# Attention start-up of a fused attention and expert kernel: exponentials from PSUM, q, v and probability loads and POOL steps in another order

## The chip, the cores and the metric

The kernel runs on one core of a Trainium2 chip. The metric is the device time of one execution in microseconds; three runs of the kernel before are shown, and their median counts.

## The reference

Three stages in float32, on 2304 tokens of 512 features.

```python
k_p = k.reshape(B, H, Sp, 8, D).mean(axis=3)      # B, H, S, D = 4, 8, 576, 64; Sp = 72
v_p = v.reshape(B, H, Sp, 8, D).mean(axis=3)
scores = scale * q @ k_p.T                          # scale = 1/sqrt(D)
attn = exp(scores - max); attn /= sum + 1e-9
x = attn @ v_p                                      # as (2304, 512)
for e in range(4): out += p[:, e] * (relu(x @ w1[e]) @ w2[e])   # p = domain_probs / their sum
a, b = out @ g_w1, out @ g_w2; result = (a * b @ w3) @ w_out
```

## The kernel before

Tokens are worked in 18 tiles of 128, three tiles to a block of 384. The first block's attention is the start-up: nothing of the experts can run before it. From then on the matmuls of expert 0 (units of one 128-column chunk of w1, made by `expert_h` and followed two units later by the matmuls with w2) fill TensorE, and the attention of the later blocks is spread between them as small pieces, in lists called `hooks`. `hooks[n]` runs after half-unit n: `hooks[0]` after unit 0, `hooks[2]` after unit 1, and so on.

The program is scheduled by hand: every engine executes its instructions in the order in which the Python code emits them, and waits in that order. `lead` (L640) is the start-up as a list of pieces. Its parts are:

- `warm(n)`: n transposes of the identity on TensorE, into a PSUM bank that nobody reads.
- `do_k` (`pool_k`, L415 to L420): VectorE sums eight rows of k, POOL multiplies by a mask. `do_kT` (`make_kT`, L428, L430): TensorE transposes, ScalarE evicts.
- `do_qT(t)` (`make_qT`): for the first three tiles TensorE transposes q (L479), VectorE (L482) or ScalarE (L484) evicts; for later tiles VectorE alone transposes (L487).
- `do_scores(t)` (L500): eight matmuls into two PSUM banks, four heads in each.
- `do_exps(t)`: per bank the maximum on VectorE (L512), then for tiles 0 and 1 the scaled negated maximum on VectorE (L514) and four exponentials on ScalarE straight from PSUM (L516); for tile 2 and all later ones a subtraction on VectorE (L518) and one exponential of 288 columns on ScalarE (L519).
- `do_normalise(t, eng)`: the sums on VectorE (L525 to L527), then the product with their reciprocals (L530), on POOL or VectorE.
- `do_v`: POOL pools a head of v with three additions (L440 to L442); heads 5 to 7 are pooled on TensorE (`pool_v_pe`, L448).
- `do_turn(t)` (`attn_T`): TensorE transposes the probabilities, four heads at a time (L539); ScalarE evicts (L545), for the second half of tile 2 VectorE (L543).
- `do_attend(0)` (L554): the matmuls with v; ScalarE and VectorE split the result in a high and a low part (L175, L176).
- `weight(eng)`: takes the oldest expert weight from a ring of four buffers, ScalarE writes its high part (L175), `eng` its low part (L176), and SP issues the load of the next weight into a free buffer (L194, L196).

All loads are issued by SP in program order. First come those in `first`: k of batch 0 in five pieces (L399), q tiles 0 to 2 (L457), v heads 0 to 7 (L404); then four expert weights, the domain probabilities (L1088), and as space allows q tiles 3 and 4 (L469) and k of batch 1. The probabilities are normalised by `probs` (L619 to L622) in `hooks[7]`.

Of the kernel before, what the change touches and what calls it, by code (L numbers as in the profile page):

```python
# [11 lines left out]
AF = mybir.ActivationFunctionType  # L12
ALU = mybir.AluOpType
AX = mybir.AxisListType
# [3 lines left out]
def fused_kernel(  # L18
# [16 lines left out]
    nc = tc.nc  # L35
    PSUM = bass.MemoryType.PSUM

    B, H, S, D = q.shape
    POOL = 8
    NK = S // POOL  # L40
    NT, DM = out.shape
    E, _, F = moe_w1.shape
    P = 128
# [10 lines left out]
    NCH = (NROW + P - 1) // P  # L54
    TAIL = NROW - (NCH - 1) * P
    assert D == 64 and H * D == DM and NB * BLK == NT and 2 * HB == S and TAIL <= P and KC == 4 and FC == 8
    LOGIT = 1.0 / (POOL * D ** 0.5)
# [10 lines left out]
    LEAD = 3  # L68
# [73 lines left out]
    dp = p_area[:, :NTILE * E].rearrange("p (t e) -> p t e", e=E)  # L142
# [184 lines left out]
    with tc.manual_schedule():  # L327
# [16 lines left out]
        def bank(name):  # L344
            turn[0] += 1
            return spare[(turn[0] - 1) % len(spare)](name)
# [46 lines left out]
        in_t, kb_t, kT_t, vp_t, qT_t, sc_t, e_t, sm_t, at_t = {}, {}, {}, {}, {}, {}, {}, {}, {}  # L393
# [29 lines left out]
        def make_kT(b, g0, g1):  # L423
            if g0 == 0:
                kT_t[b] = ap.tile([P, NCH * P], F32, tag="kT", name="kT")
            pt = bank("kT_ps")
            for c in range(g0, g1):
                nc.tensor.transpose(pt[:, (c - g0) * P:(c - g0 + 1) * P],  # L428
                                    kb_t[b][:, c].rearrange("p a d -> p (a d)"), ident)
            nc.scalar.activation(kT_t[b][:, g0 * P:g1 * P], pt[:, :(g1 - g0) * P], AF.Copy)  # L430

        def pool_v(b, h, eng):
            if h == 0:
# [39 lines left out]
        def make_qT(t):  # L473

            if t < LEAD:
                r = in_t.pop(("q", t))
                pt = bank("qT_ps")
                for hp in range(NP):
                    nc.tensor.transpose(pt[:, hp * P:(hp + 1) * P], r[:, hp * P:(hp + 1) * P], ident)  # L479
                qT = acc_lead[0][:, t, :].rearrange("p (a b) -> p a b", b=P)  # L480
                if t == 0:
                    nc.vector.tensor_copy(qT.rearrange("p a b -> p (a b)"), pt)  # L482
                else:
                    nc.scalar.activation(qT.rearrange("p a b -> p (a b)"), pt, AF.Copy)  # L484
            else:
                qT = ap.tile([P, NP, P], F32, tag="qT", name="qT", bufs=1)
                nc.vector.transpose(qT.rearrange("p h (j a) -> p h a j", a=4), in_t.pop(("qb", t)))  # L487
            qT_t[t] = qT
# [4 lines left out]
        def scores(t):  # L493
            qT = qT_t.pop(t)
            sc_t[t] = []
            for half in range(2):
                sc = bank("sc")
                for hp in range(2 * half, 2 * half + 2):
                    for off, n, b, s in segments(t * P, P):
                        nc.tensor.matmul(sc[off:off + n, (hp % 2) * W:(hp % 2 + 1) * W],  # L500
                                         qT[:, hp, off:off + n], kT_t[b][:, hp * W:(hp + 1) * W],
                                         start=True, stop=True)
                sc_t[t].append(sc)

        def exps(t):
            e = ap.tile([P, H, NK], F32, tag="e", name="e", bufs=3)
            mx = ap.tile([P, H], F32, tag="mx", name="mx")
            for half, sc in enumerate(sc_t.pop(t)):
                s3 = sc[:, :2 * W].rearrange("p (g j) -> p g j", j=NK)
                m = mx[:, half * G:(half + 1) * G]  # L510
                eh = e[:, half * G:(half + 1) * G]
                nc.vector.tensor_reduce(m, s3, axis=AX.X, op=ALU.max)  # L512
                if t < LEAD - 1:
                    nc.vector.tensor_scalar(m, m, -LOGIT, None, op0=ALU.mult)  # L514
                    for g in range(G):
                        nc.scalar.activation(eh[:, g], s3[:, g], AF.Exp, scale=LOGIT, bias=m[:, g:g + 1])  # L516
                else:
                    nc.vector.tensor_tensor(eh, s3, m.unsqueeze(2).broadcast_to([P, G, NK]), op=ALU.subtract)  # L518
                    nc.scalar.activation(eh, eh, AF.Exp, scale=LOGIT)  # L519
            e_t[t] = e  # L520

        def sums(t):

            sm_t[t] = ap.tile([P, H], F32, tag="sm", name="sm")
            nc.vector.tensor_reduce(sm_t[t], e_t[t], axis=AX.X, op=ALU.add)  # L525
            nc.vector.tensor_scalar(sm_t[t], sm_t[t], 1e-9, float(POOL), op0=ALU.add, op1=ALU.mult)
            nc.vector.reciprocal(sm_t[t], sm_t[t])  # L527

        def normalise(t, eng):
            eng.tensor_tensor(e_t[t], e_t[t], sm_t[t].unsqueeze(2).broadcast_to([P, H, NK]), op=ALU.mult)  # L530

        def attn_T(t, half):
            i, o = divmod(t, TPB)
            if o == 0:
                at_t[i, half] = ap.tile([P, G, BLK], F32, tag="at", name="at")
            e = e_t[t]
            pt = bank("at_ps")
            for g in range(G):
                nc.tensor.transpose(pt[:NK, g * P:(g + 1) * P], e[:, half * G + g, :], ident)  # L539
            src = pt[:NK].rearrange("p (g s) -> p g s", s=P)  # L540
            dst = at_t[i, half][:NK, :, o * P:(o + 1) * P]
            if t == LEAD - 1 and half:
                nc.vector.tensor_copy(dst, src)  # L543
            else:
                nc.scalar.activation(dst, src, AF.Copy)  # L545
# [44 lines left out]
        def do_k(b, on_pool=0):  # L590
            return [(("k", b, c), lambda c=c: pool_k(b, c, nc.gpsimd if c < on_pool else nc.vector)) for c in range(NCH)]

        def do_kT(b, cut=4):
            return [(None, lambda: make_kT(b, 0, cut)), (None, lambda: make_kT(b, cut, NCH))]

        def do_v(b, *engs):
            return [(("v", b, h), lambda h=h: pool_v(b, h, engs[h % len(engs)])) for h in range(H)]

        def do_qT(t):
            return [(("q" if t < LEAD else "qb", t), lambda: make_qT(t))] if t < NTILE else []  # L600

        def do_scores(t):
            return [(None, lambda: scores(t))]

        def do_exps(t):
            return [(None, lambda: exps(t))]

        def do_normalise(t, eng=nc.gpsimd):
            return [(None, lambda: sums(t)), (None, lambda: normalise(t, eng))]

        def do_turn(t):
            return [(None, lambda half=half: attn_T(t, half)) for half in range(2)]

        def do_attend(i):
            return [(None, lambda hp=hp: attend(i, hp)) for hp in range(NP)]
# [8 lines left out]
        def weight(eng):  # L624
            return [(None, lambda: stream.split(eng))]

        VE, GP = nc.vector, nc.gpsimd
        W0, W1, W2 = 14, 6, 6

        def warm(n):  # L630

            def f():
                pw = bank("warm")
                for _ in range(n):
                    nc.tensor.transpose(pw[:, :P], ident, ident)
            return [(None, f)]

        k0, kT0, k1, kT1 = do_k(0), do_kT(0), do_k(1, 3), do_kT(1, 3)
        v0 = do_v(0, GP)[:5] + [(None, lambda: pool_v_pe(0, 5))]
        lead = (warm(W0) + k0[:4] + kT0[:1] + k0[4:] + do_qT(0) + kT0[1:] + do_qT(1) + do_scores(0) + do_exps(0) + v0[:3]  # L640
                + do_qT(2) + do_scores(1) + do_exps(1) + do_scores(2) + do_normalise(0) + v0[3:4] + do_exps(2) + v0[5:]
                + do_normalise(1) + v0[4:5] + warm(W1) + do_turn(0) + do_normalise(2, VE) + warm(W2) + do_turn(1) + do_turn(2)
                + weight(GP) + do_qT(3) + k1[:3] + do_attend(0) + weight(VE))

        hooks = [[] for _ in range(2 * FC * ATT_BLOCKS + 11)]
        hooks[1] = k1[3:]
        hooks[7] = [(None, probs)]
        hooks[3] = kT1[:1] + do_qT(TPB + 1)
        hooks[4] = kT1[1:]
# [17 lines left out]
        for b, at_v, at_k, at_kT in ((1, 3, None, None), (2, 15, 15, 20), (3, 26, 25, 30)):  # L667
            for n, piece in enumerate(do_v(b, GP)):
                hooks[at_v + n].append(piece)
            if at_k:  # L670
                for n, piece in enumerate(do_k(b)):
                    hooks[at_k + n // 2].append(piece)
                hooks[at_kT] += do_kT(b)
        first = [("k", 0, c) for c in range(NCH)] + [("q", t) for t in range(LEAD)] + [("v", 0, h) for h in range(H)]
        loads += first + [what for what, _ in lead + sum(hooks, []) if what and what not in first]


# [407 lines left out]
            add_w2(0, n)  # L1085
        fetch(len(first))
        stream.fill()
        nc.sync.dma_start(dp, domain_probs.rearrange("(t p) e -> p t e", p=P))  # L1088
        soon = [("qb", TPB)] + [("k", 1, c) for c in range(NCH)] + [("qb", TPB + 1)]
        for piece in lead:  # L1090
            cooled(0)
# [225 lines left out]
        for half in range(2):  # L1317
            for n_b, b in enumerate(g_order):
# [29 lines left out]
                first, second = xo_t[0], xo_t[1]  # L1348
# [113 lines left out]
```

## Time and profile before

| | before |
|---|---|
| median of 3 runs | 1166.04 us (1165.78 to 1166.24) |
| profiled execution | 1165.1 us |
| its span | 1163.4 us |
| mean granted TensorE clock | 0.998 |
| busy: TensorE, VectorE, ScalarE, POOL | 1150.0, 796.7, 380.7, 484.4 us |
| DMA | 217.53 MB, mean 187 GB/s |

The span is what the profiler saw between the first and the last instruction; the time of the execution has 1.7 us around it. Times in rows are microseconds from the span's start. PE is TensorE, DVE VectorE, ACT ScalarE, SP the queue that issues DMAs. A busy TensorE is not one at its peak, as matmuls overlap.

### The profile page before, as it was taken

The numbers are of one execution on the slowest core, as the hardware profiler recorded it, in microseconds if no ns is written. First come the engines' busy times: TensorE is split into PE (matmuls) and PEld (weight loads), VectorE is DVE, ScalarE is ACT, GpSimd is POOL, SyncE is SP. The second block draws the span as 40 slices with busy tenths as digits, with TensorE's granted clock in tenths as the row PEclk, the third lists the DMA queues.
The fourth block names the chain that finished last, engine by engine and source line by source line (L and its number), as shares of the span: only waits on it lengthen the run. The fifth ranks groups of instructions, "written<-read, shape, count | busy, mean of one in ns | idle before, by whom it ended". The sixth has DMA issues, their size and how long they took to land.

```text
span 1163.4 us, 19411 instructions
## 1 busy us (share of the span) xinstructions
PE 1150.0 (99%) x6806; PEld 1041.1 (89%) x6806; DVE 796.7 (68%) x1624; ACT 380.7 (33%) x699; POOL 484.4 (42%) x563
## 2 busy tenths in 40 slices
PE   7999999999999999999999999999999999999998
PEld 6888898999898998998988989989889999999997
DVE  6866553476586778667778577877677777775454
ACT  4543433245141234421315414124352333231110
POOL 6965222166452547634446736255001222342111
PEclk9999999999999999999999999999999999999999
DMA  8956424555877645668583488686475542844651
GB/s 212 214 146 144 150 97 143 186 193 178 278 236 231 215 136 157 226 185 252 181 252 101 153 242 243 155 264 150 138 184 212 200 172 112 322 169 181 233 189 46
DMA packets 233217, 217.53 MB, mean 187 GB/s; under 512 B 92960, under 2 KB 185376, under 8 KB 233120
## 3 DMA queue, kind: packets, MB, share of 16 engines
q1 hardware_dynamic: 233120, 216.30, 60.1%
q8 instruction: 53, 0.87, 0.3%
q14 instruction: 44, 0.36, 0.1%
HBM read 144.41 MB, written 71.83 MB: 186 GB/s over the span
## 4 chain that ended last, share of the span: by engine, by line
PE 93%; DMA 2%; DVE 2%; issue 1%; ACT 1%; POOL 1%; SPq 0%; DVEq 0%; ACTq 0%; POOLq 0%
PE g L171 17%; PE g L170 17%; PE g L172 17%; PE s L170 13%; PE s L172 13%; PE s L171 13%; PE x_ps L554 1%; DMA raw<-in_moe_w_dram 1%; PE at_ps L539 1%; PE sc L500 1%; DMA stxh<-in_q_dram 1%; DMA stxl<-in_v_dram 0%; POOL plain L837 0%; PE vp_ps L448 0%; POOL w2l L176 0%
## 5 line engine op out<-in xcount | busy, mean ns | idle before, releaser
L176 POOL TENSOR_TENSOR round<-plain,round 128x576 fp32r<-128x576 f32 (+1 forms) x131 | 189.8, 1449 | 396.7 <-ACT round L175 260.0
L170 PE MATMUL s<-xo,wh 128*128 128x288 f32 x840 | 248.4, 296 | 0.0
L172 PE MATMUL s<-xo,wh 128*128 128x288 f32 x840 | 248.3, 296 | 0.0
L171 PE MATMUL s<-xo,wl 128*128 128x288 f32 x840 | 247.7, 295 | 0.0
L170 PE MATMUL g<-w2l,round 128*128 128x512 f32 x540 | 211.5, 392 | 0.0
L172 PE MATMUL g<-w2h,round 128*128 128x512 f32 x540 | 211.0, 391 | 0.0
L171 PE MATMUL g<-w2h,round 128*128 128x512 f32 x540 | 210.9, 390 | 0.1
L953 DVE TENSOR_TENSOR plain<-s,plain 128x288 f32<-128x288 f32 x320 | 137.6, 452 | 89.1 <-PE s L172 60.6
L170 PEld LDWEIGHTS s<-xo,wh 128*128 128x128 f32 x840 | 158.0, 188 | 0.9 <-DVE pb L953 0.3
L171 PEld LDWEIGHTS s<-xo,wl 128*128 128x128 f32 x840 | 157.7, 188 | 0.7
L172 PEld LDWEIGHTS s<-xo,wh 128*128 128x128 f32 x840 | 158.0, 188 | 0.0
L175 ACT ACTIVATE round<-plain 128x576 fp32r<-128x576 f32 (+1 forms) x135 | 90.9, 676 | 162.0 <-DVE plain L1311 159.0
L172 PEld LDWEIGHTS g<-w2h,round 128*128 128x128 f32 x540 | 101.3, 188 | 21.4
L170 PEld LDWEIGHTS g<-w2l,round 128*128 128x128 f32 x540 | 101.5, 188 | 20.4 <-issue 0.8
L171 PEld LDWEIGHTS g<-w2h,round 128*128 128x128 f32 x540 | 101.4, 188 | 20.1 <-DVE round L692 0.4
L1164 ACT ACTIVATE plain<-plain 128x576 f32<-128x576 f32 x96 | 65.4, 682 | 131.7 <-DVE plain L953 121.9
L955 ACT ACTIVATE plain<-s 128x288 f32<-128x288 f32 x80 | 32.2, 402 | 233.4 <-PE s L172 233.2
L288 POOL TENSOR_TENSOR x5l<-x5l 128x256 uint32<-128x256 uint32 x80 | 59.4, 742 | 99.8 <-DVE x5l L287 95.8
L953 DVE TENSOR_TENSOR plain<-s,pb 128x288 f32<-128x288 f32 x160 | 69.5, 455 | 25.8 <-PE s L172 15.5
L692 DVE SCALAR_TENSOR_TENSOR round<-g,round 128x384 fp32r<-128x384 f32 x48 | 26.6, 554 | 68.3 <-ACT round L691 68.0
L170 PE MATMUL g<-xl,round 128*128 128x384 f32 x192 | 66.6, 347 | 0.0
L172 PE MATMUL g<-xh,round 128*128 128x384 f32 x192 | 64.6, 337 | 0.0
(252 smaller groups left out, 2201.8 us busy)
## 6 DMA issues: line engine op xcount, KB each, us to landing
xo<-keptx SPq DMA_DIRECT2D x63, 576.0 KB
raw<-in_moe_w_dram SPq DMA_DIRECT2D x64, 256.0 KB
plain<-acc SPq DMA_DIRECT2D x40, 256.0 KB
keptx<-xo SPq DMA_DIRECT2D x16, 576.0 KB
x5h<-in_moe_w_dram SPq DMA_DIRECT2D x128, 64.0 KB
x5h<-in_moe_w_dram SPq DMA_DIRECT2D x32, 256.0 KB
kept<-xo SPq DMA_DIRECT2D x12, 576.0 KB
acc<-plain SPq DMA_DIRECT2D x26, 256.0 KB
```

What stands on the lines that cost most here:

```text
L170: nc.tensor.matmul(ps, lh, rl, start=first, stop=False)
L171: nc.tensor.matmul(ps, ll, rh, start=False, stop=False)
L172: nc.tensor.matmul(ps, lh, rh, start=False, stop=last)
L175: nc.scalar.activation(hi, src, AF.Copy)
L176: (lo_eng or nc.vector).tensor_tensor(lo, src, hi.bitcast(F32), op=ALU.subtract)
L288: nc.gpsimd.tensor_tensor(au, au, bu, op=ALU.add)
L500: nc.tensor.matmul(sc[off:off + n, (hp % 2) * W:(hp % 2 + 1) * W], qT[:, hp, off:off + n], kT_t[b][:, hp * W:(hp + 1) * W], start=True, st ...
L539: nc.tensor.transpose(pt[:NK, g * P:(g + 1) * P], e[:, half * G + g, :], ident)
L692: nc.vector.scalar_tensor_tensor(hl, ps, 0.0, hh.bitcast(F32), op0=ALU.max, op1=ALU.subtract)
L953: nc.vector.tensor_tensor(to, one, two, op=ALU.add)
L955: nc.scalar.activation(x, product(j, A11, B11), AF.Copy)
L1164: nc.scalar.activation(r, r, AF.Relu)
```

## The change

- k's transposes are scaled by the softmax factor as ScalarE evicts them; the exponentials carry no scale any more.
- The maxima of tiles 0 to 2 are written negated by the reduction itself. Tile 2 takes its exponentials from PSUM with a bias, eight instructions, as tiles 0 and 1 do.
- q tile 2 is evicted by VectorE instead of ScalarE.
- In `lead` each q tile's transposes stand behind the scores of the tile before; the exponentials of tile 2 stand ahead of the normalising of tile 0; the first weight's split on POOL stands ahead of v head 4; tile 2 is normalised half on VectorE (heads 0 to 3) and half on POOL (heads 4 to 7).
- v heads 0 to 2 are loaded ahead of q tile 2.
- The probabilities are loaded from `hooks[2]` and not ahead of the start-up's q and k loads.

```diff
-            nc.scalar.activation(kT_t[b][:, g0 * P:g1 * P], pt[:, :(g1 - g0) * P], AF.Copy)
+            nc.scalar.activation(kT_t[b][:, g0 * P:g1 * P], pt[:, :(g1 - g0) * P], AF.Copy, scale=LOGIT)
...
-                if t == 0:
+                if t != 1:
                     nc.vector.tensor_copy(qT.rearrange("p a b -> p (a b)"), pt)
...
-                nc.vector.tensor_reduce(m, s3, axis=AX.X, op=ALU.max)
-                if t < LEAD - 1:
-                    nc.vector.tensor_scalar(m, m, -LOGIT, None, op0=ALU.mult)
+                nc.vector.tensor_reduce(m, s3, axis=AX.X, op=ALU.max, negate=t < LEAD)
+                if t < LEAD:
                     for g in range(G):
-                        nc.scalar.activation(eh[:, g], s3[:, g], AF.Exp, scale=LOGIT, bias=m[:, g:g + 1])
+                        nc.scalar.activation(eh[:, g], s3[:, g], AF.Exp, bias=m[:, g:g + 1])
                 else:
...
-                    nc.scalar.activation(eh, eh, AF.Exp, scale=LOGIT)
+                    nc.scalar.activation(eh, eh, AF.Exp)
...
-        def normalise(t, eng):
-            eng.tensor_tensor(e_t[t], e_t[t], sm_t[t].unsqueeze(2).broadcast_to([P, H, NK]), op=ALU.mult)
+        def normalise(t, *engs):
+            n = H // len(engs)
+            for m, eng in enumerate(engs):
+                e, sm = e_t[t][:, m * n:(m + 1) * n], sm_t[t][:, m * n:(m + 1) * n]
+                eng.tensor_tensor(e, e, sm.unsqueeze(2).broadcast_to([P, n, NK]), op=ALU.mult)
...
-        lead = (warm(W0) + k0[:4] + kT0[:1] + k0[4:] + do_qT(0) + kT0[1:] + do_qT(1) + do_scores(0) + do_exps(0) + v0[:3]
-                + do_qT(2) + do_scores(1) + do_exps(1) + do_scores(2) + do_normalise(0) + v0[3:4] + do_exps(2) + v0[5:]
-                + do_normalise(1) + v0[4:5] + warm(W1) + do_turn(0) + do_normalise(2, VE) + warm(W2) + do_turn(1) + do_turn(2)
-                + weight(GP) + do_qT(3) + k1[:3] + do_attend(0) + weight(VE))
+        lead = (warm(W0) + k0[:4] + kT0[:1] + k0[4:] + do_qT(0) + kT0[1:] + do_scores(0) + do_qT(1) + do_exps(0)
+                + v0[:3] + do_scores(1) + do_qT(2) + do_exps(1) + do_scores(2) + do_exps(2) + do_normalise(0) + v0[3:4] + v0[5:]
+                + do_normalise(1) + weight(GP) + v0[4:5] + warm(W1) + do_turn(0) + do_normalise(2, VE, GP) + warm(W2)
+                + do_turn(1) + do_turn(2) + do_qT(3) + k1[:3] + do_attend(0) + weight(VE))
...
+        hooks[2] = [(None, lambda: nc.sync.dma_start(dp, domain_probs.rearrange("(t p) e -> p t e", p=P)))]
...
-        first = [("k", 0, c) for c in range(NCH)] + [("q", t) for t in range(LEAD)] + [("v", 0, h) for h in range(H)]
+        first = [("k", 0, c) for c in range(NCH)] + [("q", 0), ("q", 1)] + [("v", 0, h) for h in range(3)] + [("q", 2)] + [("v", 0, h) for h in range(3, H)]
...
-        nc.sync.dma_start(dp, domain_probs.rearrange("(t p) e -> p t e", p=P))
```

## Rows read from the trace of the kernel before

**Rows 1.** Busy time by stretch: us, PE, PEld, DVE, ACT, POOL, PEclk, DMA share, GB/s.

```profile
27.00:41.00 14.00, 12.19 (x78) 10.72 (x77) 12.72 (x23) 7.02 (x16) 12.75 (x20) 1.00 0.75 175
```

**Rows 2.** Timeline of TensorE: start, us, instructions, [idle before <-releaser].

```profile
10.82 1.60 PE L500 MATMUL sc<-ap,plain 128*128 128x144 f32 x8
12.26 0.60 PE L479 MATMUL qT_ps<-ident,stxh 128*128 128x128 f32 x4
12.70 1.15 PE L500 MATMUL sc<-ap,plain 128*128 128x144 f32 x8
15.08 1.25 PE L500 MATMUL sc<-ap,plain 128*128 128x144 f32 x8 [1.24 <-ACT plain L484]
16.66 2.79 PE L448 MATMUL vp_ps<-stxl,ident 72*72 72x192 f32 x16 [0.34 <-DMA stxl<-in_v_dram]
...
21.48 1.91 PE L539 MATMUL at_ps<-ident,ap 128*72 128x128 f32 x16
23.73 2.80 PE L554 MATMUL x_ps<-ap 72*64 72x384 f32 x16 [0.34 <-ACT ap L545]
26.46 0.44 PE L170 MATMUL g<-xl,round 128*128 128x384 f32 x1
...
56.22 1.25 PE L500 MATMUL sc<-ap 128*128 128x144 f32 x8 [0.61 <-ACT ap L545]
```

**Rows 3.** Timeline of POOL from 16 to 26 us.

```profile
16.71 1.15 POOL L530 TENSOR_TENSOR ap<-ap 128x576 f32<-128x576 f32 x1
17.82 0.72 POOL L440 TENSOR_TENSOR stxl<-stxl 72x256 f32<-72x256 f32 x1
...
19.43 1.15 POOL L530 TENSOR_TENSOR ap<-ap 128x576 f32<-128x576 f32 x1
20.54 0.73 POOL L440 TENSOR_TENSOR stxh<-stxh 72x256 f32<-72x256 f32 x1
...
22.28 0.32 POOL L442 TENSOR_TENSOR ap<-stxh 72x64 f32<-72x64 f32 x1
24.27 1.28 POOL L176 TENSOR_TENSOR round<-raw,round 128x512 fp32r<-128x512 f32 x1 [1.68 <-ACT round L175]
```

**Rows 4.** Timeline of VectorE from 9 to 24 us.

```profile
9.98 0.69 DVE L482 COPY plain<-qT_ps 128x512 f32<-128x512 f32 x1 [0.98 <-PE qT_ps L479]
...
12.54 0.45 DVE L512 TENSOR_REDUCE ap<-sc 128x4 f32<-128x288 f32 x1
...
17.68 0.74 DVE L525 TENSOR_REDUCE ap<-ap 128x8 f32<-128x576 f32 x1
...
18.78 0.71 DVE L525 TENSOR_REDUCE ap<-ap 128x8 f32<-128x576 f32 x1
...
20.88 1.01 DVE L530 TENSOR_TENSOR ap<-ap 128x576 f32<-128x576 f32 x1
23.42 0.69 DVE L543 COPY ap<-at_ps 72x512 f32<-72x512 f32 x1 [1.54 <-PE at_ps L539]
```

**Rows 5.** DMA queues, packets of two stretches: 18 to 22 us and 36 to 56 us.

```profile
DMA packets 2501, 0.56 MB, mean 139 GB/s; under 512 B 2020, under 2 KB 2422, under 8 KB 2500
...
DMA packets 4424, 4.48 MB, mean 224 GB/s; under 512 B 384, under 2 KB 3204, under 8 KB 4419
q1 hardware_dynamic: 4419, 4.43, 99.3%
```

**Rows 6.** Timeline of ScalarE: a q eviction, exponentials of tile 0, a late weight.

```profile
11.05 0.60 ACT L484 ACTIVATE plain<-qT_ps 128x512 f32<-128x512 f32 x1 [0.58 <-PE qT_ps L479]
12.73 1.80 ACT L516 ACTIVATE ap<-sc,ap 128x72 f32<-128x72 f32 x8 [1.08 <-DVE ap L514]
...
54.49 0.63 ACT L175 ACTIVATE round<-raw 128x512 fp32r<-128x512 f32 x1 [0.84 <-DMA raw<-in_moe_w_dram]
```

**Rows 7.** SP's timeline: the issue behind the probabilities' DMA, and a v load.

```profile
15.06 4.45 SPq L469 DMA_DIRECT2D stxh<-in_q_dram  x1
...
39.26 0.33 SPq L404 DMA_DIRECT2D stxh<-in_v_dram  x1
```

More of the change, by code (lines that the diff above doesn't have):

```diff
@@ L606, in do_exps, with do_normalise @@
             return [(None, lambda: exps(t))]
-        def do_normalise(t, eng=nc.gpsimd):
-            return [(None, lambda: sums(t)), (None, lambda: normalise(t, eng))]
+        def do_normalise(t, *engs):
+            return [(None, lambda: sums(t)), (None, lambda: normalise(t, *(engs or (nc.gpsimd,))))]
         def do_turn(t):
```

## The prediction

> **What bounds the kernel now.** I read the busy times first: TensorE leaves 13.4 us of the span idle (table above), so only that can be won. It lies in the start-up, ahead of the first expert matmul at 26.46 us, and in a few later gaps: 1.81 us between 27 and 41 us (14.00 less 12.19) [rows 1] and 0.61 us at 56.22 us [rows 2]. Behind that the tensor engine's timeline shows none. So the change is worth what it moves TensorE at about 57 us.
>
> Next I read the start-up engine by engine. TensorE [rows 2] does the scores of tiles 0, 1 and 2 (10.82, 12.70, 15.08), waits 0.34 us for the last v loads, pools v (16.66), turns the probabilities of the three tiles (to 23.39), attends (23.73) and reaches the experts. The stretch from 16.66 on is a fixed amount of work, filled with warm-up transposes, as long as each tile's normalised exponentials are there in time. They are: POOL normalises tile 0 at 16.71 and tile 1 at 19.43 [rows 3], VectorE tile 2 at 20.88 [rows 4], while TensorE turns tiles 1 and 2 only from 21.48. POOL runs without a hole from 16.71 to 22.60; its order is the thing to watch.
>
> Between 27 and 41 us VectorE is the full one (12.72 of 14 us) [rows 1]; the DMA engines are full between 36 and 56 us (99.3%, 224 GB/s) [rows 5], and the gap at 56.22 goes back to ScalarE, which waited 0.84 us for an expert weight [rows 6].
>
> **The scores in their new order.** Each q tile's transposes now follow the scores of the tile before, so its eviction stands open on the path. From [rows 2, 4, 6]:
> - Scores 0 start at 10.82 as before (the q copy on VectorE ends at 9.98 + 0.69 = 10.67). After 1.44 us (10.82 to 12.26) come the four transposes of q tile 1, 0.60, to 12.86.
> - Their eviction on ScalarE, 0.60, ends at 13.46. Scores 1 take 1.15: 13.5 to 14.65.
> - The transposes of q tile 2 overlap the scores' tail by 0.16 (12.70 against 12.26 + 0.60) and end at 15.09. q tile 2 now lands behind three v loads: at most 3 x 144 KB at 224 GB/s = 1.9 us after the 12.26 at which it was used before, 14.2, in time.
> - The copy on VectorE, 0.69, ends at 15.8. Scores 2 take 1.25: to 17.05, where they ended at 16.33.
>
> v pooling on TensorE then starts at 17.05 instead of 16.66, whether or not the last v loads come 0.34 us sooner. That is +0.4 and would be all, if the rest followed.
>
> **The exponentials.** ScalarE takes 1.80 us for a tile's eight [rows 6], starting at 13.46 behind the q eviction. The maximum of tile 1 is queued on VectorE behind the copy of q tile 2: 15.8 + 0.45 [rows 4], so tile 1 runs 16.3 to 18.1 and tile 2 to 19.9. VectorE's sums of tile 2 take 1.10 (17.68 to 18.78) and its half of the product half of 1.01: 21.5, ahead of its use. Four small multiplications and two subtractions less on VectorE, the maximum written negated and the scale at k's eviction cost nothing here: nothing waits for the removed ones, and an ACTIVATE with a scale is what each exponential already was. The bound for k's eviction is 0 to one more eviction, 0.60; I take 0.
>
> **POOL's queue.** This decides. VectorE now sums tile 0 only after the maxima of tile 2, which need scores 2: 17.05 + 0.45 + 1.10 = 18.6. POOL, idle by then although v came early, goes on in its order [rows 3]: normalise 0 (1.11), v head 3 (1.61), normalise 1 (1.11), the weight's low half, moved ahead (1.28), v head 4 (1.61), and only then its half of normalise 2 (0.57): 18.6 + 7.29 = 25.9. TensorE must turn that half (0.5) before it attends: 26.4 instead of 23.73, **+2.7 us**. All of POOL's steps but the last were off the path before.
>
> v head 4 is priced from two rows. It took 2.06 us (20.54 to 22.60) where VectorE's product with two SBUF operands ran beside it [rows 3, 4] and head 3 took 1.61; I take 1.61, because VectorE is nearly through with its product by then, and keep 2.06 (+0.45) for the range. The Trainium skill (SBUF — State Buffer, Who interferes with whom) says that such a VectorE instruction contends with a GpSimd instruction that reads SBUF. The trace agrees for head 4; by the rule the sum would be +3.1 where they meet, and +2.7 where they don't.
>
> The new half-microsecond hole ahead of scores 0 may make TensorE slower for the work behind it. Bound: 0 to the 0.5 us, rounded up, by which scores 0 (1.60) exceeded scores 1 (1.15) [rows 2]; I take 0, as scores 1 and 2 behind a hole of 1.24 us ran alike.
>
> **From 27 to 57 us.** VectorE's copy of the late half moves from 23.42 to 26.4 [rows 4], +3.0. VectorE is nearly full to 41 us and gives back at most its 1.28 us of idle time [rows 1]; I take 0.5, as most of that idle time waits for TensorE, which is late itself. So TensorE is some 2.5 us late at 41 us (bounds 0.9, were all its 1.81 given back, and 3.0). At 56.22 the 0.61 us of waiting for a weight vanishes under the delay, if the weight comes as before: **+1.9**.
>
> **The probabilities' DMA.** It moves from ahead of the q load of tile 3 to the hook after expert unit 1, past that load, four k loads, q tile 4 and the first v loads of batch 1 on SP's queue. Before, between 18 and 22 us, the engines moved 0.56 MB with 2020 packets under 512 bytes; at 224 GB/s these 4 us would carry 0.90 MB, so it cost (0.90 - 0.56) / 0.224 = 1.5 us [rows 5]. SP's next issue was held 4.45 us, to 19.5 [rows 7]. Early, both were hidden: none of TensorE's waits in the start-up ends with a load issued behind it [rows 2]. Late, it stands on SP just ahead of the v load that was issued at 39.26 [rows 7], in the full stretch, and queued behind it are v loads and the two w1 weights whose landing held ScalarE. Bounds 0 and 4.45; I take 1.5, plus the 0.4 by which POOL frees weight buffers later (25.9 for 25.55): the weights land **+1.9** late.
>
> The two paths meet at 56 us, and the later one decides, which lies a little above either: +2.2. What SP saves early is worth nothing later, since its next weight loads wait for buffers; the weight that is split earlier on POOL has its refill queued behind the same loads.
>
> **The sum.** The profiled execution took 1165.1 us, so it would be 1167.3. It lies 0.94 under the median of the three runs; against that median of 1166.04 the forecast is **1168.2 us**. A measurement of this kernel can tell 0.2%, 2.33 us, from no change: the line is at 1168.4.
>
> **Rivals.**
> - **Absorbed.** The late start is given back: all 1.81 us of idle time before 41 us and the 0.61 at 56 close, and the DMA finds holes. 2.7 - 2.42 = +0.3, with the bounds 0 to 1.3: about 1166.4. For it: the k transposes of batch 1 waited for POOL, which is hardly later. Against it: VectorE is full there.
> - **SP is held.** The load's 2304 rows of four floats hold SP for 4.45 us at 39 us, so the weights land 4.45 + 0.4 = 4.9 late: 1170.9. For it: this is what happened to the load behind them before. Against it: the queue may be shorter there.
> - **POOL is in time, not slower.** If the sums of tile 0 come by 16.1 (23.4 less 7.29), POOL's half is ready when TensorE gets there. Then v's earlier landing counts: the 0.34 wait goes, and some of the later gaps with the earlier loads, -0.4 to -2.7, say -0.8: 1165.2. The point that decides is scores 2 ending by 14.6; against it stand the two open evictions.
>
> That the probabilities come too late for their own use belongs to the second: VectorE needs them behind several units of work, and would wait.
>
> **How the numbers follow.** Late POOL half 0.53 (1167.3 to 1169.4, about 0.25 of it over the line), absorbed 0.20, SP held 0.17, in time 0.10 (half of it beyond the line). Faster 0.05, same 0.28 + 0.20 + 0.05 = 0.53, slower 0.25 + 0.17 = 0.42. The range leaves out the early rival below 1165.4 and the tail above 1171.2, the held SP's 1170.9 being in it.
>
> **What would show it.** Right: scores 2 ending near 17, POOL's half of normalise 2 starting after 25, attention on TensorE near 26.4, the first expert matmul near 29; the gap at 56 us gone or filled by the late weight; a stretch of small packets at 39 to 46 us. Wrong: POOL's half done before 23.5, or TensorE at 57 us no later than before. If attention is late and the total the same, the absorbed rival holds.

## The result and the profile after

The changed kernel takes 1173.84 us (median of 4 runs, 1173.29 to 1174.82) against 1165.91 us: a ratio of 1.0072, 95% interval 1.006 to 1.0084, some 8 us slower. The forecast of 1168.2 us had the sign and missed the size, and the range ended at 1171.2. The profiled execution took 1173.29 us, its span 1171.3 us.

The timeline of TensorE in the changed kernel, where [rows 2] stood before (start, us, instructions, idle before and what ended it):

```profile
8.55 1.06 PE L479 MATMUL qT_ps<-ident,plain 128*128 128x128 f32 x4
...
10.48 2.26 PE L500 MATMUL sc<-ap,plain 128*128 128x144 f32 x8 [0.66 <-DVE plain L482]
12.54 1.06 PE L479 MATMUL qT_ps<-ident,stxh 128*128 128x128 f32 x4
14.28 1.25 PE L500 MATMUL sc<-ap,plain 128*128 128x144 f32 x8 [0.69 <-ACT plain L484]
15.37 0.60 PE L479 MATMUL qT_ps<-ident,stxl 128*128 128x128 f32 x4
16.75 1.25 PE L500 MATMUL sc<-ap,plain 128*128 128x144 f32 x8 [0.78 <-DVE plain L482]
...
23.73 1.07 PE L541 MATMUL at_ps<-ident,ap 128*72 128x128 f32 x8 [0.94 <-POOL ap L532]
25.36 0.60 PE L541 MATMUL at_ps<-ident,ap 128*72 128x128 f32 x4 [0.57 <-DVE ap L532]
27.40 0.63 PE L541 MATMUL at_ps<-ident,ap 128*72 128x128 f32 x4 [1.44 <-POOL ap L532]
27.96 5.39 PE L556 MATMUL x_ps<-ap 72*64 72x384 f32 x16
```

Scores 2 end at 18.0 and not at 16.3; TensorE then waits three times for normalised exponentials, last for POOL's half. The second number of the last line is the surprise: the same 16 attention matmuls take 5.39 us, 2.80 before. The busy times by stretch (us; PE, PEld, DVE, ACT, POOL; granted clock, DMA share, GB/s) tell why. The last row has the whole stretch of [rows 1]:

```profile
25.00:27.00 2.00, 0.60 (x4) 0.37 (x4) 0.21 (x1) 1.06 (x2) 1.84 (x4) 1.00 0.87 144
27.00:29.00 2.00, 1.60 (x8) 0.90 (x10) 0.93 (x2) 0.00 (x0) 1.80 (x4) 0.73 0.51 88
29.00:31.00 2.00, 2.00 (x8) 0.71 (x6) 1.31 (x2) 0.66 (x2) 1.80 (x4) 0.50 0.30 69
...
35.00:37.00 2.00, 2.00 (x8) 2.00 (x8) 0.13 (x1) 0.00 (x0) 0.00 (x0) 0.50 0.38 92
37.00:39.00 2.00, 2.00 (x12) 2.00 (x11) 0.95 (x2) 1.48 (x3) 0.00 (x0) 0.71 0.10 39
39.00:41.00 2.00, 2.00 (x14) 1.97 (x13) 1.93 (x6) 0.50 (x2) 1.29 (x1) 1.00 0.17 49
27.00:41.00 14.00, 13.60 (x54) 9.78 (x55) 7.46 (x14) 4.46 (x9) 7.21 (x14) 0.63 0.28 71
```

After TensorE had worked 0.60 of 2 us (25 to 27) and then the four transposes at 27.40, the granted clock fell, at about 27.9 us, to 0.50, its lower level of 1.2 GHz. It stayed there to about 38 us although TensorE had no gap in those ten microseconds. Attention and the first expert unit ran at half speed, the scores of tile 3 in part (1.58 us for 1.14). Before, that stretch had 1.00 [rows 1].

Further on, TensorE waits once more, for VectorE's transpose of a later q tile: 0.77 us before (first row), 1.76 us in the changed kernel (second row). Its other waits up to 57 us (0.57, 0.46 and 0.61 us before) are gone.

```profile
38.90 1.20 PE L500 MATMUL sc<-ap 128*64 128x144 f32 x16 [0.77 <-DVE ap L487]
```

```profile
47.66 1.20 PE L500 MATMUL sc<-ap 128*64 128x144 f32 x16 [1.76 <-DVE ap L487]
```

With these rows the loss of the profiled execution adds up. Attention starts 4.23 us late (27.96 less 23.73), the scores of tile 3 are 8.61 us late (37.28 less 28.67), so the low level between them costs 4.38; behind them TensorE waits 1.76 us instead of 2.41. That makes 7.96 us, and the spans differ by 7.9 (1171.3 less 1163.4).

POOL, where [rows 3] stood, and VectorE's product:

```profile
19.80 1.15 POOL L532 TENSOR_TENSOR ap<-ap 128x576 f32<-128x576 f32 x1 [4.49 <-DVE ap L526]
...
22.52 1.15 POOL L532 TENSOR_TENSOR ap<-ap 128x576 f32<-128x576 f32 x1
23.63 1.27 POOL L176 TENSOR_TENSOR round<-raw,round 128x512 fp32r<-128x512 f32 x1
24.86 0.94 POOL L440 TENSOR_TENSOR stxh<-stxh 72x256 f32<-72x256 f32 x1
...
26.68 0.66 POOL L532 TENSOR_TENSOR ap<-ap 128x288 f32<-128x288 f32 x1
```

```profile
22.47 2.75 DVE L532 TENSOR_TENSOR ap<-ap 128x288 f32<-128x288 f32 x1
```

POOL sits idle for 4.49 us until the sums of tile 0 arrive, then works through the queue as forecast and reaches its half at 26.68. VectorE's half, priced at half of 1.01 us [rows 4], takes 2.75 us, beside POOL's normalise 1 and weight.

### The profile page after: what moved, and what is told of

Same layout as the page of the kernel before. It is cut to its first block, busy times and chain, and to the rows that moved or that the text cites. A ratio compares the mean times of both kernels' runs of the same rounds, so it can differ in the third digit from the quotient of the medians.

```text
span 1171.3 us, 19416 instructions
## 1 busy us (share of the span) xinstructions
PE 1155.9 (99%) x6806; PEld 1044.7 (89%) x6806; DVE 797.5 (68%) x1619; ACT 380.8 (33%) x704; POOL 483.9 (41%) x564
## 4 chain that ended last, share of the span: by engine, by line
PE 94%; DVE 2%; POOL 1%; issue 1%; DMA 1%; ACT 1%; SPq 0%; DVEq 0%; POOLq 0%; ACTq 0%
PE g L171 17%; PE g L170 17%; PE g L172 17%; PE s L170 13%; PE s L171 13%; PE s L172 13%; PE x_ps L556 2%; PE sc L500 2%; PE at_ps L541 1%; DMA stxh<-in_v_dram 0%; DMA plain<-in_k_dram 0%; POOL w2l L176 0%; POOL plain L840 0%; ACT wh L175 0%; PE qT_ps L479 0%
```

## The experiments

All were timed against the kernel before on the same chip. Ratios with their 95% intervals:

| run | median us (range) | over before |
|---|---|---|
| changed kernel | 1173.84 (1173.29 to 1174.82) | 1.0072 (1.006 to 1.0084) |
| e1 | 1172.34 (1168.29 to 1173.54) | 1.0055 (1.0042 to 1.0067) |
| e2 | 1170.08 (1169.13 to 1175.85) | 1.0048 (1.0032 to 1.0064) |
| e3 | 1173.27 (1169.75 to 1174.05) | 1.0061 (1.0049 to 1.0074) |
| e4 | 1170.09 (1167.23 to 1172.71) | 1.0041 (1.003 to 1.0053) |
| e5 | 1165.93 (1163.79 to 1167.82) | 1.0000 (0.9991 to 1.0009) |
| e6 | 1168.76 (1167.94 to 1171.88) | 1.0027 (1.0016 to 1.0037) |
| e7 | 1169.24 (1167.94 to 1169.88) | 1.0025 (1.0015 to 1.0035) |
| e8 | 1166.48 (1165.60 to 1170.03) | 1.0006 (0.9998 to 1.0015) |
| e9 | 1168.62 (1166.18 to 1169.55) | 1.0024 (1.0015 to 1.0033) |
| e10 | 1166.74 (1165.32 to 1169.28) | 1.0008 (0.9999 to 1.0017) |
| e11 | 1164.97 (1164.09 to 1166.38) | 0.9995 (0.9986 to 1.0004) |
| e12 | 1166.24 (1164.91 to 1168.11) | 1.0005 (0.9996 to 1.0013) |

The intervals of e1, e2 and e3 overlap with that of the changed kernel; those of e4 to e12 lie under it.

### e1: tile 2 wholly on VectorE

```diff
- do_normalise(2, VE, GP)
+ do_normalise(2, VE)
```

> The changed kernel with tile 2 normalised wholly on VectorE again. Theory A (TensorE waits for POOL's half at 25.36 and 27.40, drops to its lower clock level and runs attention and the first units at half speed until 38 us): VectorE's product, which starts at 22.5, shares its time with POOL and ends at 25.2 to 25.7, attention starts at 26.2 to 26.5 instead of 27.96; TensorE still idles some 2 us, so the clock may or may not fall: 1167.5 to 1169.5 if it stays up, 1171 to 1173 if it falls. Rival B (the late half alone, with no part for the clock): 1.5 us less than the changed kernel, 1172. Rival C (the late probabilities' load): no difference, 1173.8.

1172.34 us, with single runs from 1168.29. In the profiled execution the durations of TensorE's instructions show the low level elsewhere, from the scores to the turning of tile 0, although the column of the granted clock says 1.00 there (its timeline):

```profile
14.63 2.29 PE L500 MATMUL sc<-ap,plain 128*128 128x144 f32 x8 [0.69 <-ACT plain L484]
...
18.55 2.29 PE L500 MATMUL sc<-ap,plain 128*128 128x144 f32 x8 [0.78 <-DVE plain L482]
20.63 5.33 PE L448 MATMUL vp_ps<-stxl,ident 72*72 72x192 f32 x16
...
32.19 2.80 PE L556 MATMUL x_ps<-ap 72*64 72x384 f32 x16 [0.34 <-ACT ap L547]
```

Scores 1 and 2 take 2.29 us each, v pooling 5.33 and not 2.79, and attention, at full speed, starts at 32.19 us. Rival B's figure is met, but by another way than it says: no half was late here; in this execution the loss was clock. Taking away POOL's half alone cures little: the open evictions of q leave holes of their own, 0.69 and 0.78 us here, and e9 shows what filling them brings.

### e2: the waits at the turning filled

```diff
- warm(W2) + do_turn(1) + do_turn(2)
+ warm(14) + do_turn(1) + warm(5) + do_turn(2)[:1] + warm(12) + do_turn(2)[1:]
```

> The changed kernel with 25 more warm-up transposes on TensorE, put where it waits for normalised exponentials (8 ahead of tile 1's turning, 5 and 12 ahead of the halves of tile 2); nothing comes earlier. Theory A: the granted clock stays at its full level from 27 to 38 us, attention takes 2.8 us and not 5.4, the first expert unit 2.4 and not 4.2: some 4.5 to 5.5 us less, 1168.3 to 1169.5. Rivals B and C: no difference or a little slower, 1173.8 to 1174.5.

1170.08 us, 0.6 above theory A's figures and well under the rivals'. The profiled execution again had the low level in the scores (2.29 us each, as in e1). It was left at about 22 us, within v pooling, ahead of the filling, and behind the filling it did not come back; timeline of TensorE:

```profile
28.84 1.47 PE L637 MATMUL warm<-ident 128*128 128x128 f32 x12
30.17 0.63 PE L541 MATMUL at_ps<-ident,ap 128*72 128x128 f32 x4
30.73 2.80 PE L556 MATMUL x_ps<-ap 72*64 72x384 f32 x16
```

### e3: the probabilities early again

```diff
- hooks[2] = [(None, lambda: nc.sync.dma_start(dp, ...))]
+ nc.sync.dma_start(dp, ...)   # ahead of the start-up's q loads
```

> The changed kernel with the load of the probabilities back ahead of the start-up's q loads. Theory A: TensorE's late start is the same, and what the late load costs is hidden behind it: 1173 to 1174. Rival C (the late load holds SP for 4 us in the full stretch of the DMA and the weights come late): 1169 to 1171.

1173.27 us: no difference that could be told, as theory A has it. Rival C is out for the changed kernel. The profiled execution repeats what the changed kernel's showed: waits of 0.93, 0.56 and 1.43 us, and the low level behind them:

```profile
27.76 1.00 PE L541 MATMUL at_ps<-ident,ap 128*72 128x128 f32 x4 [1.43 <-POOL ap L532]
28.69 5.39 PE L556 MATMUL x_ps<-ap 72*64 72x384 f32 x16
```

### e4: q's transposes ahead of the scores again

```diff
- do_scores(0) + do_qT(1) + do_exps(0) + v0[:3] + do_scores(1) + do_qT(2) + do_exps(1)
+ do_qT(1) + do_scores(0) + do_exps(0) + v0[:3] + do_qT(2) + do_scores(1) + do_exps(1)
```

> The changed kernel with each q tile's transposes ahead of the scores of the tile before, as they were (all else as changed). Scores 2 end 1 to 2 us sooner, so do the sums of tile 0 and POOL's queue. Theory A: POOL's half starts at 25 instead of 26.7, TensorE still waits for it; the clock falls if what counts is the idle time that is left (1172), stays up if the shorter wait is enough (1167.5 to 1169). Rival D (the open evictions of q alone make it): 1166 to 1168.

1170.09 us, 1167.23 to 1172.71: between the cases, and widely spread. In the profiled one, the fastest, TensorE still waits 1.43 us for POOL's half, yet keeps its clock:

```profile
26.22 0.63 PE L541 MATMUL at_ps<-ident,ap 128*72 128x128 f32 x4 [1.43 <-POOL ap L532]
26.78 2.80 PE L556 MATMUL x_ps<-ap 72*64 72x384 f32 x16
```

The last wait is as long as in the changed kernel, but ahead of it TensorE waits only 0.33 us at the turning and not 0.94 and 0.57. Rival D, that q's order alone makes the loss, falls.

### e5: both undone

e1's and e4's edits together.

> The changed kernel with both of these undone: q's transposes ahead of the scores again, and tile 2 normalised wholly on VectorE. Theory A (two sources of holes in TensorE's start-up, the open evictions of q and the wait for POOL's half; each makes attention later and lets the clock fall or stay at its lower level, differently from run to run): nearly all of the loss goes, 1165.5 to 1167.5, and the runs lie within 2.5 us, as those of the kernel before do. Rival E (something else in the change, the late sums of tile 0 or the loads' order, is as large): 1169 to 1171 as with q's order alone undone.

1165.93 us, a ratio of 1.0000. It differs from e4 in POOL's half alone, so behind the late queue that half costs 0.41%, 4.8 us, as wait and clock together. Everything else in the change, the exponentials from PSUM, the scaled k, the loads' order, the late sums of tile 0 and the late probabilities, costs and brings nothing that can be told. Attention does start 0.95 us late in the profiled execution (24.68 less 23.73), and the total doesn't show it. Rival E is out.

### e6: q ahead of the scores, the waits filled

e4's and e2's edits together.

> q's transposes ahead of the scores again, POOL's half kept, and the waits at the turning filled with 25 warm-up transposes. Theory A: attention still starts 3 us late behind POOL's half (26.8), but at the full clock in nearly every run: 1166.5 to 1168.5, against 1170.1 for the same without the filling. Rival B (the clock has no part): 1170 as without the filling.

1168.76 us, a little above the range for A and 1.3 under e4; the intervals of the two ratios overlap. The profiled execution, the slowest of the nine, had the low level twice: in the scores, where scores 1 and 2 took 3.43 us (2.20 in e4), and from about 46 to 49.5 us, behind the wait for VectorE's transpose of q:

```profile
16.10 3.43 PE L500 MATMUL sc<-ap,plain 128*128 128x144 f32 x16
...
44.74 1.20 PE L500 MATMUL sc<-ap 128*64 128x144 f32 x16 [1.77 <-DVE ap L487]
```

```profile
47.00:49.00 2.00, 2.00 (x8) 2.00 (x7) 0.64 (x2) 0.80 (x2) 1.92 (x3) 0.50 0.80 80
```

So with q's order undone some 3 us are left, POOL's late half and clock together; how they share is not shown.

### e7: all holes filled

The changed kernel with e2's edit and these:

```diff
- do_scores(0) + do_qT(1) + do_exps(0)
+ warm(1) + warm(4) + do_scores(0) + do_qT(1) + warm(5) + do_exps(0)
- do_scores(1) + do_qT(2) + do_exps(1)
+ do_scores(1) + do_qT(2) + warm(6) + do_exps(1)
```

> The changed kernel as it is, with warm-up transposes in all its holes: 5 ahead of scores 0, 5 and 6 where the evictions of q tiles 1 and 2 stand open, 25 at the turning. Theory A: the clock comes up near 12 us in most runs, scores 1 and 2 take 1.25 us each and not 2.3, attention starts near 28 and runs at full clock: 1168 to 1169.5, with less spread than the 1169.1 to 1175.9 of the filling at the turning alone. Rival B: no gain from filling, 1170 or above, since transposes in the holes only add work.

1169.24 us with a spread of 1.9 us, as theory A expected. Nothing comes earlier than in the changed kernel, and attention even starts later in the profiled execution, at 28.59 against 27.96:

```profile
14.85 1.25 PE L500 MATMUL sc<-ap,plain 128*128 128x144 f32 x8
...
17.41 1.22 PE L500 MATMUL sc<-ap,plain 128*128 128x144 f32 x8 [0.22 <-DVE plain L482]
...
28.59 2.80 PE L556 MATMUL x_ps<-ap 72*64 72x384 f32 x16
...
43.83 1.20 PE L500 MATMUL sc<-ap 128*64 128x144 f32 x16 [1.75 <-DVE ap L487]
```

The work added in the holes takes 4.6 us off by the medians (1173.84 less 1169.24), 5.5 us by the ratios (0.47%), whose intervals lie apart: the clock's share, near the 4.38 us that the timeline of the changed kernel gives it. What stays, 0.25% or 2.9 us, is lateness. The last row is the wait behind which e6's execution lost its clock; here the granted clock stays at 1.00 behind it.

### e8: the kernel before, with the probabilities late

> The kernel before with the probabilities' load moved to the hook, and nothing else. By the prediction's own price it costs 1.5 us at the weights' landing (bounds 0 and 4.45), less what TensorE's 0.61 us of idle time at 56 us doesn't give: 1166.5 to 1168. Rival C (SP held for 4 us in the full stretch): 1169 to 1171. If the DMA has slack there: 1165.5.

1166.48 us against 1165.68, inside the first range; the interval takes in no difference. SP's queue, ScalarE and TensorE in the profiled execution:

```profile
40.48 0.40 SPq L647 DMA_DIRECT2D pb<-in_moe_domain_probs_dram  x1
41.06 4.61 SPq L404 DMA_DIRECT2D stxh<-in_v_dram  x1
```

```profile
54.78 0.63 ACT L175 ACTIVATE round<-raw 128x512 fp32r<-128x512 f32 x1 [1.31 <-DMA raw<-in_moe_w_dram]
```

```profile
56.60 1.25 PE L500 MATMUL sc<-ap 128*128 128x144 f32 x8 [0.79 <-ACT ap L545]
```

SP is held for 4.61 us behind the load, as the rival of the prediction said, but the weight is split at 54.78 and not 54.49 [rows 6], and TensorE waits 0.79 for 0.61 us [rows 2]. Nearly all of the hold is taken up before the weights land.

### e9: holes filled, tile 2 wholly on VectorE

e7's edits in the scores, 14 warm-ups ahead of tile 1's turning, and e1's.

> The changed kernel with q's transposes behind the scores as changed, its holes filled with warm-up transposes (5, 5 and 6, and 8 more ahead of tile 1's turning), and tile 2 normalised wholly on VectorE. Theory A: with the clock up by 12 us the open evictions themselves cost only some 1 us of lateness (scores 2 end near 18.5), and nothing waits for POOL's half: attention starts near 26, 1166.5 to 1168, against 1172.3 for the same without filling. Rival D (the order of q costs as much by the late sums as by the clock): 1169 to 1170.

1168.62 us, between A's range and rival D's, 0.6 above the first and 0.4 under the second, with runs from 1166.18. The filling takes 3.7 us off e1 (1172.34). Attention starts at 26.29 in the profiled execution, near the 26 expected and 2.6 us later than before; VectorE's whole product makes a part of that:

```profile
21.81 3.04 DVE L532 TENSOR_TENSOR ap<-ap 128x576 f32<-128x576 f32 x1
```

It took 1.01 us before [rows 4]. POOL's normalise 1 (21.87 to 23.0) and weight (22.98 to 24.2) run through this stretch, VectorE ends 0.6 us after them, and TensorE waits 0.87 us for it.

### e10: a version meant to be the best

e5 with the probabilities early.

> The changed kernel with three things undone: q's transposes ahead of the scores, tile 2 normalised wholly on VectorE, the probabilities loaded early. What is left is the exponentials from PSUM, the scaled k, q tile 2 on VectorE, v ahead of q tile 2 and the weight ahead of v head 4. If the late probabilities cost 0.8 us here as they seemed to in the kernel before: 1164.8 to 1165.5, a little under the kernel before; else 1165.5 to 1166.2.

1166.74 us, 1.0008 (0.9999 to 1.0017): missed; it is no better than the kernel before, and e8's small difference isn't confirmed by it. In the profiled execution the clock fell behind a wait for a v load (first rows; 0.50 from about 18.5 to 21.9 us). In e5 a wait of nearly the same length at the same place cost no clock (last row):

```profile
16.40 3.38 PE L448 MATMUL vp_ps<-stxl,ident 72*72 72x192 f32 x16 [1.14 <-DMA stxl<-in_v_dram]
19.58 1.49 PE L637 MATMUL warm<-ident 128*128 128x128 f32 x6
```

```profile
16.80 2.79 PE L448 MATMUL vp_ps<-stxl,ident 72*72 72x192 f32 x16 [1.05 <-DMA stxl<-in_v_dram]
```

### e11: the kernel before with short warm-ups

```diff
- W0, W1, W2 = 14, 6, 6
+ W0, W1, W2 = 14, 1, 1
```

> The kernel before with one warm-up transpose instead of six ahead of tile 0's and of tile 1's turning. If the warm-ups only fill time there, attention starts up to 0.9 us earlier, bound by ScalarE's five evictions: 1164.8 to 1165.4. If they keep the clock up, as theory A would have it for larger holes, the runs spread and the median rises: 1167 to 1170.

1164.97 us, 0.9995 (0.9986 to 1.0004): in the expected range, but a gain is not shown. Nothing shows that the clock suffers: the mean granted clock is 0.996 to 1.0 in the eleven runs, as in the runs of the kernel before, their spread is 2.3 us, and the holes at the turning are under 0.4 us each in the profiled one.

### e12: the kernel before with half of tile 2 on POOL

> The kernel before with POOL taking half of tile 2's product, and nothing else. POOL's queue starts at 16.7 there and the weight's split stands behind it, so the half is done near 23.2, when TensorE gets to it: 1165.5 to 1166.5. So the late half is made by the queue ahead of it (late sums of tile 0, the weight moved ahead), not by the split. Rival: the split product itself costs, because VectorE's half and POOL hold each other up: 1167 to 1169.

1166.24 us, 1.0005 (0.9996 to 1.0013). POOL and TensorE in the profiled execution:

```profile
23.85 0.66 POOL L533 TENSOR_TENSOR ap<-ap 128x288 f32<-128x288 f32 x1
```

```profile
24.57 0.63 PE L542 MATMUL at_ps<-ident,ap 128*72 128x128 f32 x4 [0.64 <-POOL ap L533]
25.13 2.80 PE L557 MATMUL x_ps<-ap 72*64 72x384 f32 x16
```

The wait is 0.64 us and not 1.44, and the half costs nothing that can be told. The split alone does no harm that shows; behind the queue of the changed kernel it does (e4 against e5). Of that queue's two changes, the late sums and the weight moved ahead, no run has one without the other.

## Why the prediction was wrong, and what of it held

- **The scores** were to end at 17.05; they ended at 18.0. The order of the holes was right. From the start of scores 0 to the next transposes it took 2.06 us (10.48 to 12.54) and not 1.44, the transposes took 1.06 and not 0.60, both at the low level. In the profiled execution of the kernel before that level was left during scores 0. In those of e11 and e12, with the old order, it was not (2.26 and 1.06 us as here), so the new order isn't needed for this.
- **POOL's queue** was to run from 18.6 to 25.9; it ran from 19.80 to 27.34, so its length, 7.54 against 7.29 us, was right. Attention started at 27.96 instead of 26.4: the mechanism held, but was sized too small, 4.2 us late and not 2.7.
- **The step that failed** is the one on TensorE behind a hole: "Bound: 0 to the 0.5 us ...; I take 0". It looked at the hole ahead of scores 0 alone and priced no hole behind, though the prediction itself put a wait for POOL's half ahead of attention. Behind waits of 0.94, 0.57 and 1.44 us the clock fell: attention took 2.6 us longer (5.39 less 2.80), and the scores of tile 3 moved from 28.67 to 37.28. The clock's share of the 8 us is 4.6 by e7 and 4.4 by the rows of the changed kernel, against a bound of 0.5. With that term the sum would have been 1168.2 + 4.6 = 1172.8.
- **VectorE's half** at 0.5 us was wrong (2.75), and so was the reason given for head 4's low price, that VectorE would be through: VectorE ended at 25.22, and head 4, begun at 24.86, took 1.82 us for the 1.61 priced. The half took 0.70 us in e12, where POOL pools v beside it, and 2.75 in the changed kernel beside POOL's normalise 1 and weight; the whole took 3.04 in e9, against 1.01 before. The Trainium skill's rule on the shared port (SBUF — State Buffer, Who interferes with whom) is borne out beyond what the prediction allowed it. It moved little of the total here, since POOL's half came later still.
- **From 27 to 57 us** VectorE was to be full and late. Up to 41 us it was half idle, with 7.46 us of work against 12.72 [rows 1], waiting for a slow TensorE; the work came later, and at 47.66 us TensorE waited 1.76 us for it, against 0.77. The gap at 56 us did vanish, as forecast. All together TensorE got back 0.65 us of its waits; the forecast had 0.5 and 0.61.
- **The probabilities** were priced at 1.5 us; e8 shows 0.8 by its medians and can't tell that from 0, e3 shows none. SP's hold of more than 4 us came as the second rival said, but not its effect. The 0.4 us added for POOL's weight buffers took the end of POOL's half for that of the weight's split, which the new order puts ahead: it ended at 24.90, 0.65 us sooner than before.
- **The rivals.** None held. e12 comes nearest to "POOL is in time": there TensorE waits 0.64 us for the half, and nothing shows in the total. The lateness without the clock is worth 2.9 us by e7's ratio and 3.6 by its medians (1169.24 less 1165.68), against the forecast's 2.2. So the forecast's own mechanism was there, some 1 us larger than priced, and a second one lay on top of it.

What stays open: why nearly the same wait takes the clock in some executions and not in others (e6 and e7, e10 and e5), as only profiled executions show it; and whether e11 gains half a microsecond.

## What to carry to other kernels

A wait on TensorE in a start-up is priced twice: once as the wait, and once for the clock that may fall behind it, which here cost 4.4 to 4.6 us, more than the three waits together (2.95). Before moving a step to an engine with a queue, write down what stands ahead of it in that queue and when the first of these can start. An order that lets every eviction lie beside other matmuls is worth keeping even where the sums of busy time say that little changes: q's old order alone took 0.31% off (e4).

## What the runs showed of the hardware

- The low level lasted long although TensorE was busy: from about 27.9 to 38 us in the changed kernel, without a gap from 27.96 on. In e1 it reached, by the durations, from scores 0 at 10.82 (2.26 us) over v pooling (5.33) to the turning of tile 0 at 27.03, which took 1.92 us and 1.04 in the changed kernel.
- Nearly equal waits were followed by the low level in one execution and not in another: 1.77 us in e6 but not 1.75 at the same place in e7, 1.14 us in e10 but not 1.05 in e5.
- The column of the granted clock seems to lack part of the start: it says 1.00 for 0 to 27 us in the changed kernel, while scores 0 took 2.26 us there and their neighbours 1.25. Four transposes of 128x128 take 1.06 us where the column shows 0.50, as at 9 to 10 us in the kernel before, and 0.60 us at 1.00. In a start-up the durations of equal instructions are the better witness.
- A load of 36 KB in 2304 rows of four floats held the next issue on SP for 4.45 us before, 4.61 us in e8 and 4.10 in the changed kernel. In e8 the weight behind it was split only 0.29 us later than before.
